# A list scheduler that charges VectorE and GpSimd for running at the same time

## The chip, the cores and the metric

The kernel runs on one core of one Trainium2 chip. The metric is the device time of one execution in microseconds. Before the change it is 1321.23 us, the median of three runs (1321.13 to 1322.6).

## The reference

Three stages follow one another, all in float32: attention with normalised queries and keys, a feed-forward layer with an ELU, and a gated feed-forward layer with an RMS norm ahead of it.

```python
# attention: q, k, v are (4 batches, 12 heads, 448 tokens, 64)
q_n, k_n = rmsnorm(q, g_q), rmsnorm(k, g_k)
attn = softmax(q_n @ k_n.T / sqrt(64))          # denominator + 1e-09
x = (attn @ v) laid out as (1792 tokens, 768)
# first layer: w_in is 768 x 2048, w_out 2048 x 768
h = x @ w_in
x = where(h > 0, h, exp(min(h, 0)) - 1) @ w_out
# second layer: w_gate, w_val are 768 x 1536, w_out 1536 x 768
xn = x / sqrt(mean(x * x) + 1e-06) * rms_g
g = xn @ w_gate
out = (g * sigmoid(g) * (xn @ w_val)) @ w_out
```

## The kernel before

All activations lie transposed, features on the 128 partitions and the 448 tokens of a batch along the free axis. A float32 product is made of three matmuls of a shorter format (`mm3`): each operand is split into a high part, which is a copy rounded to that format, and a low part, the operand less the high part. So every operand of a matmul costs a copy (`copy`, line 312) and a subtraction (`tt`, line 334) on some other engine. This holds for the weights (tile w, 768 columns a chunk, `w_split`), for the inputs of the layers (xs), for the activations between the two matmuls of a layer (gbig, `split_g`) and for the queries and keys (qh, ql).

The weights arrive as 64-bit words and are converted first (`w_convert`): an exact copy of the high word scaled (lines 488 and 491), the low byte (lines 498 and 501), a mask on VectorE (line 506) and a combination of two tensors in SBUF on VectorE (`stt`, line 355), into the tile wc. The first use of a chunk writes the result to memory (kept), and later uses load that.

Work comes in five stages: the first layer of batch 0, that of batch 1, the second layer of batches 0 and 1, the first layer of batches 2 and 3, the second layer of these two. The attention of batch 0 stands before them, and that of later batches is dealt out in pieces among them.

No instruction is issued where it is written. Each is handed to a planner (class `Plan`) with the engines that can do it and a price on each, in microseconds. A copy within SBUF may go to VectorE, ScalarE or GpSimd, a subtraction within SBUF to VectorE or GpSimd, lines 488 and 491 (or 498 and 501) to ScalarE or GpSimd; an operation that reads PSUM cannot go to GpSimd, and the scalar-tensor-tensor operations are VectorE's alone. Prices are formulas in the number n of columns: `0.2 + 0.0014 * n` for a VectorE operation on two SBUF tensors, `0.25 + 0.0022 * n` for such a one on GpSimd (1.94 us for 768 columns, 1.236 for 448), `0.15 + 0.00104 * n` for line 506 and for the sums of line 555.

`Plan.schedule` then runs a list schedule: it takes the engine that comes free first, and on it the ready operation that was handed in first. If the operation may go elsewhere, the engine's own time plus price plus a handicap (`WAIT`: 2.5 us for VectorE, 0.3 for ScalarE, 0.4 for GpSimd) is compared with the same for the other engines, their backlog counted at 0.6. `free[e]` is the time at which an engine has finished what it was given. The resulting start times give the order in which all instructions are issued; each engine then works through its own list in that order, held only by semaphores.

Of the kernel before, what the change touches and what calls it, by code (L numbers as in the profile page):

```python
# [17 lines left out]
PSUM = bass.MemoryType.PSUM  # L18
# [9 lines left out]
class Plan:  # L28
# [6 lines left out]
    LATE = 0.0  # L35
    DMA_LAT, DMA_RATE = 2.0, 0.3e6
    FLIGHT = 8

    def __init__(self):
        self.ops = []  # L40
        self.hist = {}
# [31 lines left out]
    def add(self, alts, outs, ins, lag=0.0, after=None, soon=False, dma=False):  # L73

        i = len(self.ops)
        preds = set() if after is None else {after}
        for aps, wr in ((ins, False), (outs, True)):
            for ap in aps:
                if ap is None:
                    continue  # L80
                name, hv, m = self.region(ap)
                h = self.hist.setdefault(name, [])
                keep = []
                for rec in h:
                    j, w, hv2, m2 = rec
                    if (hv & hv2) and (m & m2):
                        if wr or w:
                            if j != i:
                                preds.add(j)
                        if wr and not (hv2 & ~hv) and not (m2 & ~m) and j != i:  # L90
                            continue
                    keep.append(rec)
                keep.append((i, wr, hv, m))
                self.hist[name] = keep
        self.ops.append((alts, preds, lag, soon, dma))

    def schedule(self):
        n = len(self.ops)
        succ = [[] for _ in range(n)]
        npred = [len(o[1]) for o in self.ops]  # L100
        for i, o in enumerate(self.ops):
            for j in o[1]:
                succ[j].append(i)
        done = [None] * n
        ready = [0.0] * n
        eng = [None] * n
        start = [0.0] * n
        E = ["pe", "v", "a", "g", "sp"]
        free = dict.fromkeys(E, 0.0)
        fut = {e: [] for e in E}  # L110
        now = {e: [] for e in E}
        back = dict.fromkeys(E, 0.0)
        taken = [False] * n
        dma_free = 0.0
        flight = deque()

        def avail(i):
            for e in self.ops[i][0]:
                r = 0.0
                for j in self.ops[i][1]:  # L120
                    if self.ops[j][4]:
                        f = done[j] + 0.1
                    elif eng[j] == e:
                        f = done[j] - self.ops[j][2] + (0.06 if e != "pe" else 0.0)
                    else:
                        f = done[j] + self.LAT
                    r = max(r, f)
                heapq.heappush(fut[e], (r, i))

        for i in range(n):  # L130
            if npred[i] == 0:
                avail(i)
        left = n
        while left:
            best = None
            for e in E:
                while now[e] and taken[now[e][0]]:
                    back[e] -= self.ops[heapq.heappop(now[e])][0][e][0]
                while fut[e] and taken[fut[e][0][1]]:
                    heapq.heappop(fut[e])  # L140
                if now[e]:
                    t = free[e]
                elif fut[e]:
                    t = max(free[e], fut[e][0][0])
                else:
                    continue
                if best is None or t < best[0]:
                    best = (t, e)
            t, e = best
            while fut[e] and fut[e][0][0] <= t + 1e-9:  # L150
                r, i = heapq.heappop(fut[e])
                if taken[i]:
                    continue
                heapq.heappush(now[e], i)
                back[e] += self.ops[i][0][e][0]
            if not now[e]:
                continue
            i = heapq.heappop(now[e])
            alts = self.ops[i][0]
            back[e] -= alts[e][0]  # L160
            if taken[i]:
                continue
            if len(alts) > 1:
                mine = t + alts[e][0] + self.WAIT[e]
                other = min(max(free[o], t) + self.BACK * back[o] + alts[o][0] + self.WAIT[o] for o in alts if o != e)
                if other + 0.1 < mine:
                    heapq.heappush(fut[e], (t + 0.3, i))
                    free[e] = t
                    continue
            taken[i] = True  # L170
            left -= 1
            start[i], eng[i] = t, e
            free[e] = t + alts[e][0]
            if self.ops[i][4]:
                if e == "sp":
                    if len(flight) == self.FLIGHT:
                        free[e] = max(free[e], flight.popleft())
                    dma_free = max(free[e], dma_free) + self.ops[i][2]
                    done[i] = max(free[e] + self.DMA_LAT, dma_free + 0.7)
                    flight.append(done[i])  # L180
                else:
                    done[i] = free[e] + self.DMA_LAT + self.ops[i][2]
            else:
                done[i] = free[e] + self.ops[i][2]
            for s in succ[i]:
                npred[s] -= 1
                if npred[s] == 0:
                    avail(s)
        self.start_t, self.eng_t = start, eng

        late = [self.LATE if eng[i] == "sp" and not self.ops[i][3] else 0.0 for i in range(n)]
        order = sorted(range(n), key=lambda i: (start[i] + late[i], i))
        self.span = max(done)
        self.load = {e: sum(self.ops[i][0][e][0] for i in range(n) if eng[i] == e) for e in E}
        return order, eng
# [933 lines left out]
```

## Time and profile before

| | |
|---|---|
| median of 3 runs | 1321.23 us |
| profiled execution | 1322.09 us, its span 1320.3 us |
| mean granted clock of TensorE | 0.988 |
| TensorE busy | 1267.6 us (96%) |
| TensorE weight load busy | 1061.8 us (80%) |
| VectorE busy | 667.3 us (51%) |
| ScalarE busy | 645.3 us (49%) |
| GpSimd busy | 751.3 us (57%) |
| chain that ended last | TensorE 75%, VectorE 9%, transfers 5%, GpSimd 5%, no visible wait 3%, ScalarE 3% |

The span goes from the first instruction to the last. Busy is the time in which an engine had an instruction under way, as a share of the span. The chain that ended last is followed back from the last instruction, at each step to what released it. PE is TensorE, PEld its weight load, DVE VectorE, ACT ScalarE and POOL GpSimd; L355 is line 355 of the kernel. An operation is written as output<-inputs by the names of the tiles.

### The profile page before, as it was taken

The page shows a single profiled execution, that of the slowest core. Times are in us where ns is not written, and L with a number is a line of the kernel's source. Part 1 is how long each engine was busy: PE and PEld are TensorE (multiplying, and loading weights), DVE is VectorE, ACT ScalarE, POOL GpSimd, SP SyncE. Part 2 cuts the span into 40 slices and gives each one's busy share as a digit, 9 for nine tenths or more (in the row PEclk, how much of TensorE's full clock was granted, in tenths as well). Part 3 has the DMA queues.
Part 4 walks back from the last instruction along what each step waited for, and adds up shares of the span by engine and source line. Part 5 has one row for each costly group of instructions (what it writes and reads, how often), then busy time and mean ns, then how long its engine had stood idle before and what let it go on. Part 6 is the DMA issues. An engine that isn't in the chain of part 4 may idle for free.

```text
span 1320.3 us, 17649 instructions
## 1 busy us (share of the span) xinstructions
PE 1267.6 (96%) x6454; PEld 1061.8 (80%) x6454; DVE 667.3 (51%) x1085; ACT 645.3 (49%) x1263; POOL 751.3 (57%) x569
## 2 busy tenths in 40 slices
PE   4988898989999999999999999999999999999998
PEld 3546776766777777888988889999999989999998
DVE  7776989787534459754564552102121652132332
ACT  4875766677655667565544542433323533221220
POOL 2476778785655678554653663645445755453450
PEclk8899999999999999999999999999999999999999
DMA  6477877872434455644544335111112111111112
GB/s 204 143 236 245 271 245 241 267 244 81 141 118 122 133 175 185 204 154 156 167 155 145 125 123 166 48 60 48 61 48 61 48 61 48 60 49 61 48 36 84
DMA packets 62839, 173.89 MB, mean 132 GB/s; under 512 B 11024, under 2 KB 20512, under 8 KB 62752
## 3 DMA queue, kind: packets, MB, share of 16 engines
q1 hardware_dynamic: 53760, 163.31, 37.7%
q10 hardware_dynamic: 8992, 9.46, 2.7%
q8 instruction: 50, 0.82, 0.3%
q14 instruction: 37, 0.30, 0.1%
HBM read 137.56 MB, written 35.17 MB: 131 GB/s over the span
## 4 chain that ended last, share of the span: by engine, by line
PE 75%; DVE 9%; DMA 5%; POOL 5%; issue 3%; ACT 3%; ACTq 0%; SPq 0%; DVEq 0%; POOLq 0%
PE bank L295 71%; PE bank L308 4%; DVE wc L355 1%; DMA wr<-wst 1%; DMA kept<-wc 1%; DVE xs L355 1%; POOL w L340 1%; DVE bank L646 1%; POOL ql L340 1%; DVE wt L506 1%; DMA rb<-scr 1%; POOL gbig L340 1%; DVE rw L355 1%; POOL tbig L340 1%; ACT xs L363 1%
## 5 line engine op out<-in xcount | busy, mean ns | idle before, releaser
L295 PE MATMUL bank<-xs,w 128*128 128x448 f32 x2880 | 614.2, 370 | 6.3 <-DVE tbig L355 4.7
L295 PEld LDWEIGHTS bank<-xs,w 128*128 128x128 f32 x2880 | 536.5, 189 | 58.2 <-issue 7.5
L295 PE MATMUL bank<-gbig,w 128*128 128x448 f32 x2016 | 433.8, 370 | 10.6 <-ACT ybig L320 4.3
L340 POOL TENSOR_TENSOR w<-wc,w 128x768 fp32r<-128x768 f32 x159 | 303.2, 1908 | 194.2 <-ACT w L320 180.7
L295 PEld LDWEIGHTS bank<-gbig,w 128*128 128x128 f32 x2016 | 373.5, 188 | 48.4 <-issue 5.2
L320 ACT ACTIVATE w<-wc 128x768 fp32r<-128x768 f32 x100 | 84.4, 844 | 176.2 <-PE bank L295 169.8
L340 POOL TENSOR_TENSOR gbig<-tbig,gbig 128x448 fp32r<-128x448 f32 x104 | 126.6, 1218 | 68.8 <-ACT gbig L320 67.7
L646 DVE TENSOR_REDUCE bank<-bank 128x1 f32<-128x448 f32 x168 | 99.1, 625 | 62.3 <-PE bank L295 61.7
L340 POOL TENSOR_TENSOR tbig<-tbig 128x448 f32<-128x448 f32 x67 | 84.6, 1263 | 71.6 <-DVE tbig L355 64.0
L355 DVE SCALAR_TENSOR_TENSOR tbig<-tbig,bank 128x448 f32<-128x448 f32 x64 | 39.3, 617 | 144.0 <-ACT tbig L363 143.9
L324 POOL TENSOR_SCALAR w<-wc 128x768 fp32r<-128x768 f32 x68 | 59.6, 877 | 84.7 <-PE bank L295 73.9
L363 ACT ACTIVATE p<-bank,nm,rr 128x448 f32<-128x448 f32 x126 | 90.1, 719 | 17.8 <-DVE nm L647 13.5
L355 DVE SCALAR_TENSOR_TENSOR wc<-wc,wt 128x768 int32<-128x768 int32 x68 | 79.3, 1166 | 35.7 <-ACT wc L488 26.8
L320 ACT ACTIVATE pt<-bank 128x384 f32<-128x384 f32 (+1 forms) x162 | 69.3, 445 | 55.6 <-PE bank L308 46.8
L320 ACT ACTIVATE gbig<-tbig 128x448 fp32r<-128x448 f32 x94 | 54.2, 577 | 74.6 <-DVE tbig L338 41.3
L363 ACT ACTIVATE tbig<-tbig 128x448 f32<-128x448 f32 x112 | 64.4, 577 | 45.4 <-DVE tbig L338 43.2
L338 DVE TENSOR_TENSOR tbig<-bank,tbig 128x448 f32<-128x448 f32 x48 | 29.7, 620 | 98.9 <-PE bank L295 98.8
L308 PE MATMUL bank<-ident,p 128*128 128x128 f32 x441 | 72.7, 283 | 4.8 <-ACT p L363 2.5
L308 PEld LDWEIGHTS bank<-ident,p 128*128 128x128 f32 x441 | 55.1, 144 | 24.1 <-issue 5.0
L338 DVE TENSOR_TENSOR ybig<-bank,ybig 128x448 f32<-128x448 f32 x72 | 44.0, 618 | 51.7 <-PE bank L295 51.4
L355 DVE SCALAR_TENSOR_TENSOR ybig<-bank,ybig 128x448 f32<-128x448 f32 x48 | 30.0, 624 | 75.0 <-PE bank L295 75.0
L355 DVE SCALAR_TENSOR_TENSOR tbig<-tbig 128x448 f32<-128x448 f32 x48 | 53.8, 1123 | 23.3 <-ACT tbig L363 23.1
(95 smaller groups left out, 1217.5 us busy)
## 6 DMA issues: line engine op xcount, KB each, us to landing
wr<-wst SPq DMA_DIRECT2D x68, 768.0 KB
wc<-kept SPq DMA_DIRECT2D x100, 384.0 KB
kept<-wc SPq DMA_DIRECT2D x68, 384.0 KB
rw<-qk SPq DMA_DIRECT2D x21, 512.0 KB
tk<-tok SPq DMA_DIRECT2D x20, 480.0 KB
rv<-vr SPq DMA_DIRECT2D x24, 256.0 KB
out_t<-ybig SPq DMA_DIRECT2D x24, 224.0 KB
rb<-scr ACTq DMA_DIRECT2D x36, 128.0 KB
```

The lines of the kernel that those rows point to most:

```text
L295: T.matmul(o, l, r, start=start, stop=stop)
L308: T.transpose(o, i, ident)
L320: alts["a"] = (c_a(n), lambda: A.activation(out=dst, in_=src, func=AF.Copy))
L324: lambda: G.tensor_scalar(out=dst, in0=src, scalar1=1.0, scalar2=0.0, op0=ALU.mult, op1=ALU.add),
L338: alts["v"] = (c_tt(a, b, n), lambda: V.tensor_tensor(out=dst, in0=a, in1=b, op=op))
L340: alts["g"] = (0.25 + 0.0022 * n, lambda: G.tensor_tensor(out=dst, in0=a, in1=b, op=op))
L355: {"v": (c_tt(a, b, size(dst)), lambda: V.scalar_tensor_tensor(out=dst, in0=a, scalar=s, in1=b, op0=op0, op1=op1))},
L363: {"a": (c_a(size(src)) + extra, lambda: A.activation(out=dst, in_=src, func=func, **kw))},
L506: vop(0.15 + 0.00104 * WN, lambda: V.tensor_scalar(out=th, in0=h16, scalar1=0x8000, scalar2=None, op0=ALU.bitwise_and), [th], [h16])
L646: vop(c_v1(S), lambda mx=mx, ot=o[t]: V.tensor_reduce(out=mx, in_=ot, axis=AX.X, op=ALU.max, negate=True), [mx], [o[t]])
```

## The change

The planner gets a constant for VectorE (v) and for GpSimd (g). An operation is marked as shared if none of its outputs and inputs is in PSUM. When a shared operation is given to one of the two engines, its time is lengthened by the constant times the part of it that lies before the end of the last shared operation on the other engine. The operation planned earlier keeps its time. Nothing else is changed: the operations, their plain prices and the rule of choice between engines stay.

```diff
     FLIGHT = 8
+    STRETCH = {"v": 0.6, "g": 0.25}
...
-        self.ops.append((alts, preds, lag, soon, dma))
+        shared = not any(getattr(ap.tensor, "_space", None) == PSUM for ap in list(outs) + list(ins) if ap is not None)
+        self.ops.append((alts, preds, lag, soon, dma, shared))
...
         taken = [False] * n
+        port = {"v": 0.0, "g": 0.0}
...
             start[i], eng[i] = t, e
-            free[e] = t + alts[e][0]
+            price = alts[e][0]
+            if e in self.STRETCH and self.ops[i][5]:
+
+                o = "g" if e == "v" else "v"
+                price += self.STRETCH[e] * max(0.0, min(port[o], t + price) - t)
+                port[e] = t + price
+            free[e] = t + price
```

## Rows read from the trace of the kernel before

**Rows 1.** Stages: stretch, then busy us (and instructions) of each engine, clock, transfers.
```profile
0.00:99.00 99.00, 76.84 (x402) 42.93 (x404) 73.69 (x194) 69.52 (x168) 48.32 (x50) 0.91 0.60 194
99.00:330.00 231.00, 206.78 (x1054) 156.68 (x1051) 187.76 (x285) 158.23 (x322) 171.86 (x127) 0.98 0.68 228
330.00:530.00 200.00, 198.21 (x1076) 153.87 (x1075) 113.25 (x197) 129.14 (x292) 134.07 (x101) 0.99 0.47 147
530.00:792.00 262.00, 261.64 (x1345) 223.23 (x1343) 146.71 (x217) 136.33 (x238) 143.47 (x109) 1.00 0.47 153
792.00:1033.00 241.00, 241.00 (x1191) 223.32 (x1190) 48.29 (x77) 77.84 (x131) 115.52 (x88) 1.00 0.22 69
1033.00:1320.30 287.30, 283.12 (x1396) 261.75 (x1394) 97.55 (x119) 74.23 (x113) 138.06 (x99) 1.00 0.17 55
```
**Rows 2.** The chain of waits within 95 to 330 us, shares by line.
```profile
by line: PE bank L295 13.2%; issue 12.3%; DMA wr<-wst 7.4%; DMA kept<-wc 7.4%; DVE wc L355 6.1%; DMA rb<-scr 4.3%; DVE wt L506 4.1%; POOL ql L340 3.5%; DVE bank L646 2.8%; POOL w L340 2.7%; DVE rw L355 2.6%; ACT p L363 2.4%; DMA rsb<-rsum 2
```
**Rows 3.** VectorE groups, 99 to 330 us: busy us, mean ns, idle before, releaser.
```profile
L355 DVE SCALAR_TENSOR_TENSOR wc<-wc,wt 128x768 int32<-128x768 int32 x28 | 35.6, 1270 | 5.1 <-POOL wt L501 2.9 <-ACT wt L498 1.1 <-ACT wc L488 0.3
L506 DVE TENSOR_SCALAR wt<-wr 128x768 uint16<-128x768 uint16 x28 | 32.6, 1163 | 0.2 <-DMA wr<-wst 0.2
...
L555 DVE TENSOR_REDUCE ss<-tk 128x15 f32<-128x960 f32 x13 | 14.9, 1144 | 3.0 <-ACT tk L363 2.9
...
L355 DVE SCALAR_TENSOR_TENSOR rw<-rw,gsc,rb 128x512 f32<-128x512 f32 x8 | 10.7, 1331 | 6.7 <-DMA rb<-scr 5.2 <-DMA wc<-kept 0.8 <-DMA rw<-qk 0.7
...
L338 DVE TENSOR_TENSOR w<-wc,w 128x768 fp32r<-128x768 f32 x4 | 4.3, 1072 | 0.0
...
L338 DVE TENSOR_TENSOR gbig<-tbig,gbig 128x448 fp32r<-128x448 f32 x3 | 3.8, 1251 | 0.0
```
**Rows 4.** GpSimd groups of the same stretch.
```profile
L340 POOL TENSOR_TENSOR w<-wc,w 128x768 fp32r<-128x768 f32 x31 | 61.3, 1978 | 3.7 <-DMA kept<-wc 1.2 <-ACT w L320 0.7
L501 POOL TENSOR_SCALAR wt<-wr 128x768 uint16<-128x768 uint8 x21 | 23.2, 1106 | 14.2 <-DVE wc L355 12.9
...
L340 POOL TENSOR_TENSOR gbig<-tbig,gbig 128x448 fp32r<-128x448 f32 x14 | 20.5, 1464 | 4.3 <-ACT gbig L320 3.8
L324 POOL TENSOR_SCALAR w<-wc 128x768 fp32r<-128x768 f32 x16 | 14.1, 881 | 7.5 <-DVE wc L355 3.7 <-PE bank L295 2.2 <-DVE rr L355 1.0
L491 POOL TENSOR_SCALAR wc<-wr 128x768 f32<-128x768 f32 x10 | 11.1, 1115 | 5.1 <-DVE ybig L338 1.9 <-DMA wr<-wst 1.9 <-DVE rr L349 1.1
```
**Rows 5.** Timeline, 140 to 152 us: start us, duration us, instruction, idle before.
```profile
145.11 2.10 POOL L340 TENSOR_TENSOR w<-wc,w 128x768 fp32r<-128x768 f32 x1
145.43 2.25 DVE L506 TENSOR_SCALAR wt<-wr 128x768 uint16<-128x768 uint16 x1
...
148.63 0.94 DVE L355 SCALAR_TENSOR_TENSOR wc<-wc,wt 128x768 int32<-128x768 int32 x1
...
150.75 0.61 DVE L506 TENSOR_SCALAR wt<-wr 128x768 uint16<-128x768 uint16 x1
150.83 2.21 POOL L340 TENSOR_TENSOR w<-wc,w 128x768 fp32r<-128x768 f32 x1
...
151.50 2.36 DVE L355 SCALAR_TENSOR_TENSOR wc<-wc,wt 128x768 int32<-128x768 int32 x1
```
**Rows 6.** GpSimd groups from 792 to 1023 us.
```profile
L340 POOL TENSOR_TENSOR w<-wc,w 128x768 fp32r<-128x768 f32 x31 | 57.3, 1848 | 68.3 <-ACT w L320 63.9 <-DMA wc<-kept 3.0
L340 POOL TENSOR_TENSOR gbig<-tbig,gbig 128x448 fp32r<-128x448 f32 x31 | 35.8, 1153 | 41.9 <-ACT gbig L320 41.9
```
**Rows 7.** ScalarE groups, 99 to 330 us: copies that GpSimd could do.
```profile
L320 ACT ACTIVATE w<-wc 128x768 fp32r<-128x768 f32 x18 | 15.2, 842 | 6.7 <-DVE wc L355 6.4 <-PE bank L295 0.3
...
L498 ACT ACTIVATE wt<-wr 128x768 uint16<-128x768 uint8 x8 | 8.7, 1084 | 2.8 <-DMA wr<-wst 1.7 <-DVE wc L355 1.1
```
**Rows 8.** TensorE groups of the same stretch.
```profile
L295 PE MATMUL bank<-xs,w 128*128 128x448 f32 x342 | 81.3, 384 | 5.6 <-DVE tbig L355 4.7 <-POOL xs L340 0.7
L295 PE MATMUL bank<-gbig,w 128*128 128x448 f32 x288 | 68.4, 380 | 9.5 <-ACT ybig L320 4.3 <-DVE tbig L355 2.1 <-POOL gbig L340 1.7
```

## The prediction

> **What bounds the kernel now.** I read the table of stages first. From 330 us on TensorE is busy in 198.2 of 200, 261.6 of 262, 241.0 of 241 and 283.1 of 287.3 us: there it is the bound, and at most 1.8 + 0.4 + 4.2 = 6.4 us of idle time is left to win. From 0 to 99 us it is idle for 22 us and from 99 to 330 us for 24 us [rows 1]. The change deals in VectorE and GpSimd operations, so I look for the stage where these two are full: it is the second, with VectorE at 187.8 of 231 us (81%) and GpSimd at 171.9 (74%), while ScalarE is at 158.2 (69%); in the first stage GpSimd is at 49%, from 530 us on VectorE is at 56% or less [rows 1].
>
> Then the chain of waits of that second stretch: matmuls of line 295 are 13.2% of it, and the rest is a mixture of transfers (7.4% twice), VectorE (6.1, 4.1 and 2.8%) and GpSimd (3.5 and 2.7%) [rows 2]. No one engine bounds this stage; work is handed on between them, and what lengthens each link counts.
>
> Then the groups of instructions on VectorE there. The two steps of the weight conversion run 28 times each, at 1270 ns (line 355) and 1163 ns (line 506) [rows 3]. The timeline shows the same two much shorter: 0.94 us at 148.63 and 0.61 us at 150.75 [rows 5]. The long cases have one pattern: at 145.43 line 506 begins 0.32 us into a GpSimd subtraction (145.11 to 147.21) and ends at 147.68, 0.47 us after it; at 151.50 line 355 begins inside the next one (150.83 to 153.04) and takes 2.36 us, while the line 506 that began before that subtraction kept its 0.61 [rows 5]. So an operation of one engine that meets one of the other stands nearly still until the first is done. For these two forms that costs 28 x (1.27 - 0.94) + 28 x (1.163 - 0.61) = 9.2 + 15.5 = 24.7 us. On GpSimd a weight subtraction takes 1978 ns there against 1848 in a later stage where VectorE has little to do, and one of gbig 1464 against 1153 [rows 4, 6]: 31 x 0.13 + 14 x 0.311 = 8.4 us.
>
> With these waits taken out, GpSimd's work is about 163.5 us and that of the two conversion steps 28 x 1.55 = 43.4; rw and the subtractions of w and gbig on VectorE add up to 18.8 us with their waits [rows 3, 4]. If meeting operations nearly exclude each other, this is 207 to 226 us of a 231 us stage. That is the limit of the stage as I read it: not either engine, but the two together.
>
> **The change, part by part.** It adds, removes and resizes no operation. In the planner, a VectorE operation without a PSUM operand is lengthened by 0.6 of its overlap with the last such GpSimd operation that is under way, a GpSimd one by 0.25 of the overlap the other way; the later of the two pays. The comparison between engines still uses the plain price, so a choice changes only through the later time at which an engine is free.
>
> Term 1, copies and conversions that leave GpSimd for ScalarE. The ones that may go are 21 of line 501, 16 of line 324 and 10 of line 491: 23.2 + 14.1 + 11.1 = 48.4 us [rows 4]. How many go I estimate from the load that the planner now believes in: the VectorE groups that count are 35.6 + 32.6 + 10.7 + 4.3 + 3.8 = 87 us, 38% of the stage [rows 3]; in about half of the meetings GpSimd is the later, so its 172 us grow by 0.25 x 0.38 x 0.5, some 5%, or 8 us. A copy that moves takes 1.03 us off GpSimd (48.4 / 47) and puts 0.84 to 1.08 on ScalarE [rows 7]; the two balance again after 8 / (1.03 + 0.95), about 4 copies. Ends: none moves, 0; half of the 47 move, -24 us of GpSimd time, more than the stage's idle TensorE time gives back. ScalarE has 73 us free, so a move hides there. I take 4 x 1.03 = -4 us, near the lower end because that is where the load estimate lies.
>
> Term 2, subtractions that go from VectorE to GpSimd, because VectorE is charged more. In the stage VectorE does 4 of w and 3 of gbig [rows 3]; on GpSimd they take 1.85 and 1.15 us [rows 6]; what they take on VectorE without a wait I estimate from the undisturbed line 355, as wide as a weight subtraction, at 0.94 us [rows 5], and 0.55 for 448 of 768 columns. Ends: 0, and 4 x 0.91 + 3 x 0.60 = +5.4 us if all go. A subtraction going the other way gains as much. I take +1, about one subtraction: the planner's own handicap for VectorE leaves few of them there to be moved.
>
> Term 3, order. An operation that is planned with the duration it will have is followed by the right neighbour; one planned too short leaves its engine, which runs in order, waiting at the wrong instruction. The planned price of the gbig-sized subtraction on GpSimd is 1.236 us against 1.464 measured, that of line 506 is 0.95 against 1.163; that of line 355 is 1.275 against 1.270 [rows 3, 4]. So prices go the right way for some and past the truth for others. What order can win at once is where TensorE waits for VectorE or GpSimd: 4.7 + 0.7 us before the xs products and 2.1 + 1.7 before the gbig ones, 9.2 us [rows 8]. Ends: -24 us (all idle TensorE time of the stage) and +10 (as much again as these waits). I take a half of the 9.2, -4.5, since two of three prices get nearer to the measurement.
>
> Term 4, the other stages. In the first, few of these operations run; after 330 us TensorE covers what is moved, and if that cover is gone, a late operand shows up as idle TensorE time. Ends -6 (the 6.4 us left) and +8 (four cases of some 2 us, the length of a weight subtraction); I take 0.
>
> Sum: -4 + 1 - 4.5 + 0 = -7.5 us. The profiled execution took 1322.09 us, of which 1320.3 are the span; that gives 1314.6, and as the median of the runs shown is 0.86 us lower, **1314 us** for the median.
>
> The Trainium skill (SBUF — State Buffer, section "Who interferes with whom") says that VectorE and GpSimd share a pair of ports as an exclusive lock, and that the one that comes second is blocked entirely until the first has finished. The rows at 145.43 and 151.50 agree [rows 5]. By that rule a collision costs the whole remainder rather than 0.6 or 0.25 of it, and no order shortens the sum of both engines' work in a full stage; then only terms 1 and 2 count, which is the first rival. The same section says that a tensor_reduce never contends on this chip; the trace agrees, with 1144 ns for line 555 in the crowded stage [rows 3] beside a planned 1.148 us, and the planner now lengthens it all the same, which speaks for the second rival.
>
> **The rivals.** First, no change: the order is different and the sum of both engines' work in the full stage is the same, because few copies move; terms 1 and 2 cancel and term 3 is nothing. For it: 207 to 226 of 231 us are filled whatever the order. Against it: the chain of waits there is a mixture [rows 2], so order should count. Time 1319 to 1323.
>
> Second, slower: the waits are counted twice. The planned 1.275 us of line 355 is already the measured mean of 1270 ns with its waits [rows 3], and 0.6 of a full overlap makes it 2.04; the 13 sums of line 555 cannot be disturbed and are lengthened too. The planner then believes VectorE and GpSimd to be later than they are, gives ScalarE more than it can take between the exponentials, and pushes the 7 subtractions to GpSimd. Price: term 2 in full, +5.4, and for some ten moved copies standing ahead of an exponential or an eviction that TensorE waits for half a copy each, 10 x 0.45 = +4.5: about 1331. It decides from the point where ScalarE's busy time in the stage passes some 170 us while GpSimd's doesn't fall.
>
> Third, a large gain: the order was the main fault, and half of the 46 idle us of the first two stages goes: 1300. For it: 24.7 us of waits in two forms alone. Against it: those waits come from load, and load stays.
>
> **How the numbers follow.** Forecast (a gain of 3 to 13 us) 0.38; large gain 0.12; no change 0.17; slower 0.33. The sign is uncertain because an order from a list schedule is sensitive to any price. The forecast alone would be 1308 to 1318; the range that takes in the rivals is 1302 to 1332, with about one case in ten beyond each end. Faster or slower by over 0.2% (2.6 us, about what a measurement of this kernel can tell from none): 0.50 faster, 0.17 within, 0.33 slower.
>
> **What would show it.** Right: in the stage that ends near 330 us, lines 324, 491 and 501 on GpSimd lose about 4 instructions and ScalarE gains them; lines 355 and 506 have lower means than 1270 and 1163 ns; TensorE passes 630 products of xs and gbig with w [rows 8] some 7 us earlier; after that the table of stages is as before. Wrong: the same counts with the same time (first rival); more subtractions on GpSimd and more ScalarE time, with TensorE waiting for evictions (second); or new idle time of TensorE after 530 us, which I have priced at nothing.

## The result: slower by 0.67%

The changed kernel takes 1333.61 us (median of 7 runs, 1329.85 to 1335.39), the kernel before beside it 1322.6 us (7 runs). The medians are 11.0 us apart; the ratio on record, from all these runs, is 1.0067, with a 95% interval of 1.005 to 1.0084. The two profiled executions read below differ by 10.8 us in their spans. The forecast was 1314 us in a range of 1302 to 1332: the sign is wrong, and the time lies above the range.

### The profile page after: what moved, and what is told of

Its sections match the earlier page's. It is cut to its first block, busy times and chain, and to the rows that moved or that the text cites. A ratio compares the mean times of both kernels' runs of the same rounds, so it can differ in the third digit from the quotient of the medians.

```text
span 1331.1 us, 17653 instructions
## 1 busy us (share of the span) xinstructions
PE 1268.5 (95%) x6454; PEld 1061.4 (80%) x6454; DVE 659.2 (50%) x1079; ACT 648.4 (49%) x1267; POOL 754.4 (57%) x571
## 4 chain that ended last, share of the span: by engine, by line
PE 75%; DMA 8%; DVE 6%; POOL 4%; issue 3%; ACT 3%; ACTq 1%; SPq 0%; DVEq 0%; POOLq 0%
PE bank L304 72%; PE bank L317 3%; DMA wr<-wst 3%; DMA rsb<-rsum 1%; DMA rsum<-rt 1%; POOL ql L349 1%; DVE wt L515 1%; POOL w L349 1%; DMA kept<-wc 1%; DVE wc L364 1%; ACTq L385 1%; DVE sn L347 1%; POOL gbig L349 1%; DMA rw<-qk 1%; DVE tbig L364 1%
## 5 line engine op out<-in xcount | busy, mean ns | idle before, releaser
L349 POOL TENSOR_TENSOR gbig<-tbig,gbig 128x448 fp32r<-128x448 f32 x109 | 132.1, 1213 | 65.4 <-ACT gbig L329 64.5
L333 POOL TENSOR_SCALAR w<-wc 128x768 fp32r<-128x768 f32 x71 | 61.4, 866 | 90.7 <-PE bank L304 73.6
L347 DVE TENSOR_TENSOR ybig<-bank,ybig 128x448 f32<-128x448 f32 x72 | 44.3, 621 | 55.5 <-PE bank L304 55.3
L515 DVE TENSOR_SCALAR wt<-wr 128x768 uint16<-128x768 uint16 x68 | 69.3, 1019 | 0.5 <-DMA wr<-wst 0.4
```

What stands on the lines that cost most here:

```text
L333: lambda: G.tensor_scalar(out=dst, in0=src, scalar1=1.0, scalar2=0.0, op0=ALU.mult, op1=ALU.add),
L347: alts["v"] = (c_tt(a, b, n), lambda: V.tensor_tensor(out=dst, in0=a, in1=b, op=op))
L349: alts["g"] = (0.25 + 0.0022 * n, lambda: G.tensor_tensor(out=dst, in0=a, in1=b, op=op))
L515: vop(0.15 + 0.00104 * WN, lambda: V.tensor_scalar(out=th, in0=h16, scalar1=0x8000, scalar2=None, op0=ALU.bitwise_and), [th], [h16])
```

## The profile after

The changed kernel's stages (columns as in [rows 1]). The first cut stays at 99 us and the later ones lie 11 us behind those of [rows 1]; each stage then holds as many TensorE instructions as there, give or take 8:

```profile
0.00:99.00 99.00, 72.52 (x394) 41.07 (x394) 73.76 (x191) 67.84 (x167) 43.83 (x46) 0.93 0.54 179
99.00:341.00 242.00, 213.01 (x1058) 158.32 (x1057) 183.85 (x281) 163.50 (x327) 169.11 (x127) 0.96 0.67 222
341.00:541.00 200.00, 196.75 (x1075) 153.05 (x1076) 107.86 (x199) 129.07 (x295) 129.78 (x99) 1.00 0.45 142
541.00:803.00 262.00, 261.76 (x1344) 223.18 (x1342) 149.99 (x219) 135.87 (x239) 155.56 (x115) 1.00 0.49 159
803.00:1044.00 241.00, 241.00 (x1189) 223.39 (x1190) 47.06 (x76) 77.34 (x130) 116.36 (x89) 1.00 0.22 68
1044.00:1331.10 287.10, 283.48 (x1399) 262.36 (x1397) 96.67 (x119) 74.80 (x114) 139.76 (x100) 1.00 0.18 56
```

From 341 us on each stage is as long as before and TensorE about as full, so the 11 us are lost ahead of that point. With these cuts they show in the second stage, 242 us instead of 231, but TensorE is behind already at 99 us, with 394 instructions against 402. Over the first two stages together TensorE is idle for 55.5 us instead of 46.4: 9 of the 11 us are waiting. The other 2 are more busy time, at a mean granted clock of 0.96 against 0.98 in the second stage, both near the upper of its two levels, so the clock explains little of the loss.

The second stage is longer although VectorE is busy for 4 us less in it (183.9 against 187.8) and GpSimd for 3 us less (169.1 against 171.9). So it is not the sum of the two engines' work that lengthened it. What grew is TensorE's waiting. Its first three groups there, to be read against [rows 8], and the third of them before:

```profile
L304 PE MATMUL bank<-xs,w 128*128 128x448 f32 x342 | 78.7, 376 | 4.4 <-POOL xs L349 2.8 <-POOL xs L333 1.3 <-ACT tbig L372 0.3
L304 PE MATMUL bank<-gbig,w 128*128 128x448 f32 x288 | 71.0, 389 | 11.1 <-POOL gbig L349 4.6 <-DVE tbig L364 2.5 <-DVE w L347 2.2
L317 PE MATMUL bank<-ident,p 128*128 128x128 f32 x126 | 21.6, 283 | 8.0 <-ACT pt L329 6.2 <-ACT p L372 1.8
```
```profile
L308 PE MATMUL bank<-ident,p 128*128 128x128 f32 x126 | 21.1, 280 | 3.9 <-ACT p L363 2.5 <-ACT pt L320 1.4
```

The waits for VectorE and GpSimd before the xs and gbig products, 9.2 us before, are 2.8 + 1.3 + 4.6 + 2.5 + 2.2 = 13.4 us now. Those before the transposes of the attention (ident, p) went from 3.9 to 8.0 us.

The groups of that stage on GpSimd, then on VectorE, then on ScalarE, to be read against [rows 3, 4, 7]:

```profile
L349 POOL TENSOR_TENSOR w<-wc,w 128x768 fp32r<-128x768 f32 x32 | 62.2, 1946 | 14.2 <-ACT w L329 12.6 <-DMA wc<-kept 0.3
L349 POOL TENSOR_TENSOR gbig<-tbig,gbig 128x448 fp32r<-128x448 f32 x15 | 19.7, 1310 | 0.4 <-ACT gbig L329 0.2
...
L510 POOL TENSOR_SCALAR wt<-wr 128x768 uint16<-128x768 uint8 x14 | 15.0, 1071 | 10.6 <-DMA wr<-wst 5.3 <-DVE wc L364 4.6
L500 POOL TENSOR_SCALAR wc<-wr 128x768 f32<-128x768 f32 x12 | 13.9, 1159 | 0.4
L333 POOL TENSOR_SCALAR w<-wc 128x768 fp32r<-128x768 f32 x15 | 13.6, 906 | 10.3 <-DVE wc L364 3.4 <-DMA wr<-wst 2.4 <-DMA wc<-kept 2.1
```
```profile
L364 DVE SCALAR_TENSOR_TENSOR wc<-wc,wt 128x768 int32<-128x768 int32 x29 | 36.6, 1262 | 0.6
L515 DVE TENSOR_SCALAR wt<-wr 128x768 uint16<-128x768 uint16 x29 | 31.0, 1069 | 0.0
...
L347 DVE TENSOR_TENSOR w<-wc,w 128x768 fp32r<-128x768 f32 x2 | 3.1, 1548 | 0.1
...
L347 DVE TENSOR_TENSOR gbig<-tbig,gbig 128x448 fp32r<-128x448 f32 x2 | 1.8, 892 | 0.0
```
```profile
L329 ACT ACTIVATE w<-wc 128x768 fp32r<-128x768 f32 x20 | 16.8, 840 | 5.7 <-DMA scr<-rr 2.5 <-DVE wc L364 2.5 <-DMA wc<-kept 0.7
L507 ACT ACTIVATE wt<-wr 128x768 uint16<-128x768 uint8 x15 | 16.2, 1082 | 8.8 <-DVE wc L364 7.2 <-DVE ybig L347 1.6
```

Copies and conversions did move to ScalarE (47 on GpSimd became 14 + 12 + 15 = 41), and waits at the collisions shrank: line 506, now 515, went from 1163 to 1069 ns. The change did what it says, and more time went elsewhere.

Where: in the attention of batch 1, whose six pairs (6 to 11) are worked on one after another in this stage. It cannot begin before the sums of squares of all six (line 555, now 564) and the factors made of them (13 VectorE operations on 128x90). Lines of the timeline of before (start, duration, instruction):

```profile
29.39 1.14 DVE L555 TENSOR_REDUCE ss<-tk 128x15 f32<-128x960 f32 x1
...
32.01 1.29 DVE L355 SCALAR_TENSOR_TENSOR rw<-rw,gsc,rb 128x512 f32<-128x512 f32 x1
...
104.23 1.15 DVE L555 TENSOR_REDUCE ss<-tk 128x15 f32<-128x960 f32 x1 [1.23 <-ACT tk L363]
...
119.78 1.08 DVE L355 SCALAR_TENSOR_TENSOR rr<-sn,rr 128x90 f32<-128x90 f32 x1
...
131.39 0.75 DVE L355 SCALAR_TENSOR_TENSOR rw<-rw,gsc,rb 128x512 f32<-128x512 f32 x1 [5.17 <-DMA rb<-scr]
...
322.08 0.62 DVE L338 TENSOR_TENSOR xf<-bank,rsb 128x448 f32<-128x448 f32 x1 [2.18 <-PE bank L295]
```

and of the changed kernel:

```profile
33.14 1.74 DVE L364 SCALAR_TENSOR_TENSOR rw<-rw,gsc,rb 128x512 f32<-128x512 f32 x1 [2.27 <-POOL qh L333]
...
37.82 1.15 DVE L564 TENSOR_REDUCE ss<-tk 128x15 f32<-128x960 f32 x1
...
112.19 1.15 DVE L564 TENSOR_REDUCE ss<-tk 128x15 f32<-128x960 f32 x1
113.38 0.21 DVE L358 TENSOR_SCALAR ss<-ss 128x90 f32<-128x90 f32 x1
...
121.73 1.87 DVE L364 SCALAR_TENSOR_TENSOR rr<-sn,rr 128x90 f32<-128x90 f32 x1
...
132.46 0.24 DVE L364 SCALAR_TENSOR_TENSOR rr<-sn,rr 128x90 f32<-128x90 f32 x1
...
140.73 0.75 DVE L364 SCALAR_TENSOR_TENSOR rw<-rw,gsc,rb 128x512 f32<-128x512 f32 x1 [0.36 <-DMA rb<-scr]
...
334.72 0.62 DVE L347 TENSOR_TENSOR xf<-bank,rsb 128x448 f32<-128x448 f32 x1 [6.22 <-PE bank L304]
```

Before, VectorE does the sum of pair 6 at 29.39 and then the keys of pair 2 (rw); after, the keys go first and the sum follows at 37.82. All later sums share one tile, tk, so the next load (issued at 31.68, now at 38.99) and every sum behind it shift too. The last one comes 8.0 us later (104.23, 112.19), the factors are done at 132.7 instead of 120.9, the keys of pair 6 at 140.7 instead of 131.4, and the output of pair 11 is taken from PSUM at 334.72 instead of 322.08: 12.6 us, and the span is 10.8 us longer. From that point the kernel before needs 998.2 us to its end and the changed one 996.4.

## The experiments

Times are ratios to the kernel before, measured beside it on the same chip, by 4 to 12 runs of each new kernel. "Factors" is the end of batch 1's factors, "pair 11" the start of its eviction, both in us of the profiled execution.

| run | ratio (95%) | factors | pair 11 |
|---|---|---|---|
| before | 1 | 120.9 | 322.1 |
| lock | 1.0014 (0.9997 to 1.003) | 122.9 | 327.4 |
| lat201 | 1.0021 (0.9997 to 1.0044) | 124.3 | 325.7 |
| choice_only | 1.0097 (1.006 to 1.0134) | 124.7 | 327.4 |
| g_only | 1.0031 (1.0015 to 1.0048) | 127.4 | 326.5 |
| no_sums | 1.0038 (1.002 to 1.0055) | 128.9 | 327.7 |
| order_only | 1.012 (1.0101 to 1.0139) | 129.9 | 339.7 |
| late_b | 1.0075 (1.0045 to 1.0105) | 130.9 | 333.3 |
| the change | 1.0067 (1.005 to 1.0084) | 132.7 | 334.7 |
| v_only | 1.0074 (1.0053 to 1.0096) | 134.2 | 333.9 |
| tiny | 1.0103 (1.0078 to 1.0127) | 134.7 | 335.3 |
| early_b, early_a, early_tiny | 1.0019, 1.0025, 1.0016 | 97.0, 98.4, 97.8 | 320.1, 307.3, 321.8 |
| earlier_b, earlier_b2 | 0.9983, 1.0006 | 73.6, 74.3 | 305.9, 306.6 |
| earlier_a, earlier_tiny | 1.0011, 1.0022 | 74.8, 72.6 | 311.1, 316.8 |

**Order or engines.** Two kernels run the planner twice and take the engines from one plan and the order from the other.

```diff
-        order, eng = self.schedule()
+        self.STRETCH = {"v": 0.0, "g": 0.0}    # choice_only: 0.6, 0.25
+        eng = self.schedule()[1]
+        self.STRETCH = {"v": 0.6, "g": 0.25}   # choice_only: 0.0, 0.0
+        order = self.schedule()[0]
```

> Engines as the planner chose them without the stretch, order of all instructions as planned with it. If the engine choices made the kernel slower (7 subtractions to GpSimd, ScalarE too full): about 1322 us, as before. If the order did: about 1333 us. If any new combination is a fresh draw with no direction: 1322 to 1340, not the sum of anything.

> Engines as chosen with the stretch, order as planned without it. If the engine choices are the cause: about 1333 us. If the order is: about 1322 us. The two parts should add up to the 11 us of the whole change if they act separately; if it is a fresh draw, both can be slower than the whole.

Measured 1339.35 and 1335.57 us, beside 1324.55 for before: 1.012 and 1.0097, each at least as slow as the whole change. So the two do not add up, and neither half by itself is the cause. That an order made for one set of engines does not fit another is a likely reading, which no run shows.

**How little is enough.** The stretch is 0.01 on both engines.

> Stretch of 0.01 on both engines: no planned duration moves by more than 1%. If waits counted twice are the cause, the effect shrinks with the constant, to under 0.5 us: 1322 us. If the list schedule flips engine choices at any small disturbance and the time is a draw, it differs from before by several us, up or down: 1315 to 1340.

Measured 1336.38 us, 1.0103: no smaller than with 0.6 and 0.25, and inside the range that was given for a mere draw. The loss does not follow the size of the charge. The factors come at 134.7 us.

**Prices near to the trace.** Plain prices as measured without overlap, and the whole remainder as the wait. The cuts below leave out that sums and reciprocals are not charged, and that the prices of the mask and of GpSimd's operations are lowered too.

```diff
-                price += self.STRETCH[e] * max(0.0, min(port[o], t + price) - t)
+                price += max(0.0, port[o] - t)
...
-        return 0.2 + 0.0014 * n if two_sbuf(a, b) else c_v1(n)
+        return c_v1(n)
```

> Planned durations of shared operations set to what the trace shows where nothing overlaps (0.95 us for 768 columns on VectorE, 0.61 for line 506's mask, 1.85 on GpSimd), and a shared operation that meets one of the other engine waits for its whole remainder; sums and reciprocals are not shared. If waits counted twice made the plan worse, this plan is nearer to the chip than both and takes 1322 us or less. If the accuracy of prices is not what decides, it lands like any other draw, 1322 to 1340.

Measured 1326.65 us, 1.0014 with an interval that holds 1. The loss is mostly gone, but the 1322 us or less that were expected if a better model gives a better plan did not come. Its factors come at 122.9 us. One plan cannot tell a better model from an order that happens to keep the start of batch 1 early.

**An earlier start for batch 1.** Loads and sums of batch 1 are handed in during batch 0's attention, so the planner, which takes what was handed in first, no longer fills them into gaps.

```diff
         for i in range(NPB + 1):
...
+                if i < NPB and u == 3:
+                    load_tk(NPB + i)
+                    squares(NPB + i)
+                    if i == NPB - 1:
+                        factors(1, 0, NPB)
...
-        for i in range(NPB, 2 * NPB):
-            load_tk(i)
-            squares(i)
-        factors(1, 0, NPB)
```

> Without the stretch; the loads and squares of batch 1's six pairs are handed in during the attention of batch 0, one pair each round, and its factors right after, instead of behind it. Theory: the attention of batch 1 is one chain that begins with these factors and ends with the evicted output of pair 11, at 322 us before, and the span is that time plus 997 us; the scaled keys of pair 6 then come at 120 us or earlier instead of 131, and the time falls by 5 to 15 us, to about 1312. Rival, that the time is a draw at any change of order: 1320 to 1340.

> The same earlier hand-in with the stretch of 0.6 and 0.25. Theory: the start of the chain is what the stretch had delayed (scaled keys of pair 6 at 140.7 us), so most of the 11 us goes: 1310 to 1322, within 5 us of the same kernel without the stretch. If it is the engine choices or the pace of the later pairs that the stretch spoils: still some 10 us slower than that kernel.

> The same earlier hand-in with a stretch of 0.01. Theory: with the chain's start handed in early, a tiny disturbance can no longer push it back, so 1308 to 1320. Rival, a draw: anything from 1310 to 1340.

Measured 1327.28, 1326.63 and 1326.71 us (1.0019, 1.0025, 1.0016). Two answers in one. The stretch costs nothing that can be seen here: with the other hand-in its two kernels were 11 and 12 us slower than the one without it, by their medians, and here all three are within 0.7 us. But the expected gain is missing: 1327 instead of 1312. The factors come 24 us earlier (97.0 against 120.9) and pair 11 only 2 us in early_b and 15 in early_a, and in early_a, where the attention gains most, the scaled outputs of batch 0's first layer are late in return: the last one starts at 320.40 us on ScalarE, at 304.06 before. So batch 1's attention is not the only chain that ends near here: with pair 11 early, another one sets the time. That pulling one forward pushes the other back, since both use the same engines, is a reading of early_a alone.

**A later start without the stretch.** One dependency is added: the load of pair 11's squares waits for the output of pair 5.

```diff
         for i in range(NPB, 2 * NPB):
+            if i == 2 * NPB - 1:
+                ts(tks[0][:, 0:1], r_xf.t[0][:, 0:1], 1.0, None, ALU.mult)
             load_tk(i)
```

> Without the stretch, one thing added: the load of pair 11's squares must wait for the evicted output of pair 5 (107 us before), by a one-column copy into its tile. Theory, the late start of batch 1's attention is what the stretch costs: the last sum of batch 1 comes at some 114 us instead of 105, as with the stretch (113), pair 11 is evicted some 8 us later, and the time is 1328 to 1336. Rival, pace or engine choices: the later start is made up by 322 us and the time stays within 4 us of before.

Measured 1334.07 us, 1.0075. Its timeline and its second stage:

```profile
30.70 1.14 DVE L564 TENSOR_REDUCE ss<-tk 128x15 f32<-128x960 f32 x1
...
116.86 1.15 DVE L564 TENSOR_REDUCE ss<-tk 128x15 f32<-128x960 f32 x1
...
142.92 1.38 DVE L364 SCALAR_TENSOR_TENSOR rw<-rw,gsc,rb 128x512 f32<-128x512 f32 x1 [0.27 <-DMA rb<-scr]
...
333.27 0.62 DVE L347 TENSOR_TENSOR xf<-bank,rsb 128x448 f32<-128x448 f32 x1 [6.82 <-PE bank L304]
```
```profile
99.00:341.00 242.00, 213.42 (x1056) 158.63 (x1055) 192.43 (x296) 152.01 (x307) 173.22 (x134) 0.96 0.65 218
```

The first sum is near where it was before (30.70), the last one is late (116.86), and the rest repeats the changed kernel: keys of pair 6 at 142.92, pair 11 at 333.27, the same TensorE time in the same 242 us, with another distribution of VectorE, ScalarE and GpSimd. The delay is handed on unchanged: 11.5 us at the keys of pair 6, 11.2 at pair 11, 10.9 in the span. So a later start is sufficient for the whole loss, without any charge. It is not isolated from the engines, though. The planner plans everything anew, and in this stage GpSimd now has 13 of line 510 and 24 copies of w (line 333), where before it had 21 and 16.

**A disturbance of no meaning** (the planner's latency between engines, `LAT`, is 0.201 us instead of 0.2, no stretch), and the earlier hand-in at two pairs a round, with `u in (3, 5)` in place of `u == 3`.

> No stretch; the planner's latency between engines is 0.201 us instead of 0.2, a change of no meaning. If the loss is that of any new draw of the order: 1325 to 1340, as with the stretch of 0.01. If before is an ordinary draw: within 5 us of it on either side.

> Without the stretch; the same hand-in at two pairs a round, done by the third pair of batch 0. Theory: the factors come some 10 us earlier still; if they then no longer end last, the time stays at that of one pair a round, about 1312; if the chain is still what counts, 1305.

> Stretch of 0.6 and 0.25, with the squares of batch 1 handed in two pairs a round. Theory: as at one pair a round, the stretch then costs nothing: within 4 us of 1321, the time of that hand-in without it. If it was chance that the three kernels at one pair a round agreed within 1 us: 1325 to 1335.

> Stretch of 0.01, with the squares handed in two pairs a round. Theory: within 4 us of 1321, and so 10 us or more below the same stretch in the kernel's own hand-in (1336). A draw: 1320 to 1340.

> The kernel without the stretch and with the squares handed in two pairs a round once more, in more rounds: the first time it was at 0.9983 of before, with an interval that reached to 1.0005. If that was a gain: 0.996 to 0.999 again. If it was chance: 0.999 to 1.003.

lat201: 1327.95 us, 1.0021, its start late by 3.5 us only. The time lies in both of the ranges that were to be told apart, but not every new order loses 11 us. How late batch 1 starts gives the direction and not the amount. The keys of pair 6 come at 140.0 us in no_sums, 139.8 in order_only and 140.7 in the changed kernel, and pair 11 at 327.7, 339.7 and 334.7: the pace in between also differs from plan to plan, by as much as the loss. And none of the ten new plans with the old hand-in, the change among them, is faster than before. That the kernel before is a lucky order, so that almost any new one loses something against it, is not ruled out.

Two pairs a round: 0.9983 (0.996 to 1.0005) without the stretch, 1.0006 (0.9992 to 1.002) when repeated, 1.0011 (0.9987 to 1.0036) with it and 1.0022 (1.0001 to 1.0043) with 0.01. They lie within 6 us of each other, a little more than the 4 expected. The 1312 or 1305 us that were expected of earlier_b did not come, and the small gain of its first run was not found again: no version here beats the kernel before, although pair 11 comes 5 to 16 us earlier.

**Which charge.**

> Stretch of 0.6 on VectorE alone. Theory: in the first 100 us it is VectorE's charge that keeps the sums of batch 1 waiting behind the attention of batch 0; the last of them comes at 111 to 114 us and the time is 1329 to 1337, as with both. If the GpSimd charge is what costs: within 4 us of before.

> Stretch of 0.25 on GpSimd alone. Theory: the last sum of batch 1 stays before 109 us and the time within 5 us of before (1320 to 1329). If the GpSimd charge is what costs: 1330 or more.

> Both charges, but the sums and reciprocals, which showed no wait, are not charged. If charging the sums is what delays them (part of the second rival of the prediction): last sum near 105 us and 1320 to 1326. If they are late because of what is planned before them: last sum still at 110 us or later and 1329 to 1337.

VectorE's charge alone gives the whole loss (1.0074; last sum at 113.0). GpSimd's gives 1.0031, with the last sum at 110.5, later than expected. Without the charge on sums and reciprocals the loss is about a half (1.0038), the last sum still at 107.8: neither of the two ranges came. Charging operations that show no wait (a sum takes 1147 ns in the crowded stage, 1144 before) may be a part of it, and what is planned ahead of them another; with one plan each, and halves that do not add up, the parts are not shown.

## Why the prediction was wrong

- **The bound.** Right that the second stage is where the time is lost, wrong in what limits it. "Not either engine, but the two together" does not explain a stage that grew by 11 us with 7 us less work on the two. Its end goes with the chain of batch 1's attention. In nine kernels with the old hand-in (before, the change, tiny, lock, v_only, g_only, no_sums, late_b, order_only) the span is pair 11's eviction plus 996.4 to 999.4 us; lat201 and choice_only need 1006.8 and 1006.2. late_b shows that a delay of that chain is a delay of the kernel; the early kernels, which gain nothing by an earlier one, show that the rest of the stage ends close behind it.
- **Term 1** (4 copies to ScalarE, -4 us): 6 moved. The mechanism was right, and GpSimd is busy for 2.8 us less in the stage, near to the -4 + 1 of the first two terms, though by other counts. But less work on GpSimd did not shorten the stage.
- **Term 2** (one subtraction to GpSimd, +1): 3 of 7 went from VectorE. Right in kind.
- **Term 3** (order, -4.5) is the step that failed, in sign. I argued that prices nearer to the measurement give a better order, and that it would win back a half of the 9.2 us for which TensorE waits on VectorE and GpSimd before the xs and gbig products. These waits rose to 13.4 us, and pair 11 came 12.6 us later. A charge changes who goes first wherever two operations compete, also at 29 us, a stage earlier than the one I looked at. tiny makes this plain: a charge too small to correct any price costs 12 us (1336.38 against 1324.55).
- **Term 4** (other stages, 0): right for the stages after the second. For the first I said that "few of these operations run" there; one of them, the sum at 29 us, changed its place.
- **The rivals.** "Slower" came, at 1331 against 1333.61, but not by its mechanism: ScalarE is busy for 163.5 of 242 us, not past 170, and 3 of 7 subtractions moved. So the near hit of its 1331 is luck. Its remark on the sums may hold in part (no_sums). The rule cited from the Trainium skill (SBUF — State Buffer, "Who interferes with whom") describes the collisions well, and the planner's formula doesn't follow it: it caps the overlap at the later operation's own price. A factor step of 90 columns is planned at 0.33 us and so charged with at most 0.2, and in the changed kernel one took 1.87 us against 0.24 undisturbed (121.73 and 132.46); it began inside a GpSimd subtraction that ran from 121.32 to 123.49, and ended 0.11 us after it.
- **The signs.** Two that were named for being right came: GpSimd lost copies to ScalarE, and lines 355 and 506 have lower means (1262 and 1069 ns). Both are true of a kernel that became slower, so they were signs that the charge acts and not of a gain. The third, TensorE passing the products of xs and gbig some 7 us earlier, did not come.

What stays open: why choice_only loses 1% with a start that is late by only 3.8 us. In its profiled execution 5.3 of the 13.3 us are there at pair 11, and some 5 of the rest are the slower TensorE told of in the last section, which says nothing of its other runs. Open is also whether the late start is the only cause in the change itself, where pair 11 is late by 12.6 us and the keys of pair 6 by 9.3. Shown is that a late start is sufficient, with the plan that follows from it (late_b), and that the loss is no longer seen when the start is handed in early (early_a), where another chain may hide it. The 13 factor steps, which take 19.3 us from first to last after and 13.2 before, were not tested by themselves.

## What to carry to other kernels

In a list schedule, work that is handed in late and fills gaps can be the start of the longest chain: find that start in the trace (here the last sum of the next batch) before pricing engines. Before crediting or blaming a change of a planner's costs, run it once with a hundredth of the constant; if the time moves as much, it is the order that counts and not the size of the cost. Here an engine's load in the crowded stage said little about a change that also reordered the stage ahead of it.

## What the runs showed of the hardware that was not expected

Small operations suffer most from the collisions, for their length: VectorE steps of 90 columns that take 0.24 us took up to 1.87, nearly eight times as long, while a weight conversion step of 0.94 us took 2.36 [rows 5]. And TensorE can be 2% slower with no sign of it in the granted clock. The same dense stretch of the second layer, 1100 to 1300 us, in the profiled execution of before and of lat201:

```profile
1100.00:1300.00 200.00, 200.00 (x989) 185.38 (x988) 54.35 (x71) 47.59 (x72) 92.43 (x66) 1.00 0.17 53
```
```profile
1100.00:1300.00 200.00, 200.00 (x969) 181.67 (x968) 54.16 (x69) 49.14 (x75) 93.84 (x68) 1.00 0.17 50
```

989 matmuls against 969 in 200 us, 202 against 206 ns each, both at a clock of 1.00. choice_only and early_b show the 969 too, all other profiles 988 or 989. It is not a matter of missing records, since every trace has the same 6454 TensorE instructions. Over the last 250 us that is an estimated 5 us, a part of the spread between runs of one kernel (1318.59 to 1331.58 for before). No run here says what sets it.
